# Sparse attention followed by a spectral mix: weight tiles of two modes in one transfer, strided rows of two batches in one transfer, and six modes' real parts in loads of 40 and 24 rows

## The chip, the cores and the metric

The kernel runs on one core of one Trainium2 chip. The metric is device time in microseconds (us) of one execution, as the median of several executions. "Before" is the kernel as it stood, "after" the kernel with the change.

## What is computed

The reference has two parts. Attention over `q`, `k`, `v` of shape 8 x 8 x 576 x 64 (batch, head, position, width): heads 0 to 3 see the last 32 positions (local), heads 4 to 7 see every 32nd position up to their own (strided). The result, as rows of 512, goes through a spectral layer with 64 complex weight matrices of 512 x 512 and a real one, `w_ch`:

```
X = np.fft.rfft(x, axis=1)                       # x: 8 x 576 x 512, out of the attention
Yr = einsum('bmd,mde->bme', Xr, w_r) - einsum('bmd,mde->bme', Xi, w_i)   # 64 modes m
Yi = einsum('bmd,mde->bme', Xr, w_i) + einsum('bmd,mde->bme', Xi, w_r)
y = np.fft.irfft(Y, n=S, axis=1)
u = x + y
return u + np.maximum(u @ w_ch, 0.0)
```

All inputs lie in HBM as 32-bit floats. The two weight arrays alone are 2 x 64 x 512 x 512 x 4 bytes = 134 MB; all that the profile counts as read is 163 MB.

## The kernel before, in words

**Order of the work.** One program runs on TensorE (PE), VectorE (DVE), ScalarE (ACT), GpSimd (POOL) and SyncE (SP). The order of the instructions on each engine is the order in which the Python code emits them; nothing reorders them. The stages are:

1. Strided heads (loop at line 741, 8 batches): transposes, scores, softmax, values, and half of the forward transform (`dft`, line 497). The weight tiles that have room are fetched ahead.
2. Local heads (loop at line 770, 8 batches), with the first pass of the modes between the pieces: `mode(0, m)`, m = 0 to 63, for the upper 256 of the 512 input columns.
3. Second pass of the modes, `mode(1, m)`, m = 0 to 63, for the lower 256 columns. Between the modes stand pieces of other work (`turn`, `premix`, `spec`): about one piece a mode at first, two a mode for the ten modes m = 51 to 60 (`LATE`, line 835). Modes 61 to 63 are emitted at line 948.
4. Last stage (loop at line 956): 36 units of output rows. `v_rows` (line 888) makes a row block on TensorE and ScalarE into a tile `rl`, `u_rows` (line 907) adds in VectorE into a tile `osb`, and SP sends it to HBM.

**A weight tile.** The text below counts tiles from 0 to 127: tile 64 x pass + m. A tile is `[128, 4, 512]` in 16-bit floats. Rows 0 to 63 hold the real part, rows 64 to 127 the imaginary part. Each part is one transfer of 64 rows, 8 KB read and 4 KB written a row (line 190), so a tile takes two transfers, one for `w_r` and one for `w_i`; mode 0 has no imaginary part and takes one. `mode` (line 532) does 16 small matmuls on the tile and then calls `w_fetch()` (line 551), which emits the transfers of the next tile that is not yet fetched.

**Buffers.** The pool `pw` has 11 buffers of one tile each (`NWBUF`, line 27), used in turn. Six further tiles (`GUEST`, line 169) lie in memory that is used for something else later (Y0, X0, YT). In the last stage `rl` and `osb` take turns in the same 11 buffers (lines 895 and 914).

**Queue.** The loads of weights, `q`, `k`, `v` and `w_ch` are all issued by POOL, on one queue, in the order of emission: 315 transfers in all. The program has eight completion semaphores for this queue and uses them in turn, so a transfer isn't issued before the one eight places ahead of it has landed. "Lane" below means one of those eight.

**Strided rows.** `load_str` (line 214) loads 72 rows of 8 KB for each batch and each of `v`, `q`, `k`: 64 rows in one transfer per batch, and the last 8 rows of two batches together in one. That makes 24 transfers of 64 rows and 12 of 8 x 2 rows. They go into a ring of 12 slots, three a batch, so batch b + 4 takes the place of batch b.

Of the kernel before, what the change touches and what calls it, by code (L numbers as in the profile page):

```python
# [10 lines left out]
FP = mybir.dt.float32  # L11
F16 = mybir.dt.float16
# [6 lines left out]
DM = 512  # L19
NM = 64  # L20
# [3 lines left out]
JG = [(0, 6), (6, 11), (11, 16)]  # L24
SCALE = float(1.0 / np.sqrt(D))
NEG = -30000.0
NWBUF = 11


def _host_consts():  # L30
# [49 lines left out]
def kernel(  # L80
# [10 lines left out]
    nc = tc.nc  # L91
# [3 lines left out]
    big = ctx.enter_context(tc.tile_pool(name="big", bufs=1))  # L95
# [5 lines left out]
    def psum_pools(**bufs):  # L101
        pctx.close()
        for n, c in bufs.items():
            pss[n] = pctx.enter_context(
                tc.tile_pool(name="ps_" + n, bufs=c, space=PSUM)
            )

    def psum(kind, half=False):
        if half:
            return pss[kind].tile([128, 1024], F16, tag=kind, name=kind)  # L110
        return pss[kind].tile([128, 512], FP, tag=kind, name=kind)
# [16 lines left out]
    def const_load(eng, *which):  # L128
        for n in which:
            eng.dma_start(cs[n][:, 0 : hosts[names.index(n)].shape[1]], drams[n])  # L130
# [13 lines left out]
    def spectra_tile(n):  # L144
        if n == "X0":
            Xh[0] = big.tile([128, 4, B, 2, NM], F16, tag=n, name=n)
        else:
            YS[n] = big.tile([128, 4, 4, 16, 16], F16, tag=n, name=n)

    xb = [px.tile([128, 11, 256], F16, tag="xb", name="xb") for _ in range(B)]  # L150

    pw = ctx.enter_context(tc.tile_pool(name="pw", bufs=NWBUF))
    actx = ctx.enter_context(ExitStack())
# [3 lines left out]
    ring = pat.tile([128, 12, 2048], F16, name="ring")  # L157
# [8 lines left out]

    GUEST = {3: ("Y0", 0), 4: ("Y0", 1), 5: ("X0", 0), 6: ("X0", 1)}
    GUEST |= {15: ("YT", 0), 16: ("YT", 1)}  # L170
    guests = {}
    w_tiles = []
    w_chs = {}

    def w_fetch(n=1):
        for _ in range(n):
            i = len(w_tiles)
            if i >= 2 * NM:
                return
            half, m = 1 - i // NM, i % NM  # L180
            if i in GUEST:
                n, j = GUEST[i]
                if j == 0:
                    guests[n] = big.tile([128, 2, 4, DM], F16, tag=n, name="wt")
                wt = guests[n][:, j]
            else:
                wt = pw.tile([128, 4, DM], F16, tag="w", name="wt")

            for ri, src in enumerate([moe_w_r, moe_w_i] if m else [moe_w_r]):
                nc.gpsimd.dma_start(  # L190
                    wt[ds(64 * ri, 64)],
                    src[m, ds(256 * half, 256), :].rearrange("(p c) e -> p c e", c=4),
                )
            w_tiles.append(wt)

    def w_ch_fetch():
        w_ch = pw.tile([128, 4, DM], F16, tag="w", name="w_ch")
        nc.gpsimd.dma_start(w_ch, moe_w_ch.rearrange("(c p) e -> p c e", p=128))
        w_chs["n"] = w_ch

# [3 lines left out]
    SRC = {2: v, 0: q, 1: k}  # L204
    SLOT = {2: 0, 0: 1, 1: 2}

    def str_in(b, vi):
        return ring[0:72, 3 * (b % 4) + SLOT[vi], :]
# [2 lines left out]
        t = ring[:, ds(2 * (b % 6), 2), :].rearrange("p n x -> p (n x)")  # L211
        return t[:, ds(1152 * vi, 1152)]

    def load_str(b):
        for vi in (2, 0, 1):
            nc.gpsimd.dma_start(
                str_in(b, vi)[0:64],
                SRC[vi][b, 4:8].rearrange("h (c r) d -> (h c) (r d)", r=32)[0:64],
            )
            if b % 2 == 0:  # L220
                n = 3 * (b % 4) + SLOT[vi]
                nc.gpsimd.dma_start(
                    ring[64:72, n : n + 4 : 3, :],
                    SRC[vi][b : b + 2, 4:8].rearrange(
                        "b h (c r) d -> (h c) b (r d)", r=32
                    )[64:72],
                )

    def load_loc(*bs):
        for b in bs:  # L230
            if b >= B:
                return
            for vi in (2, 0, 1):
                nc.gpsimd.dma_start(
                    loc_in(b, vi),
                    SRC[vi][b, 0:4].rearrange("h (cb i) d -> (h cb) (i d)", i=18),
                )
# [294 lines left out]
    def mode(slot, m):  # L532
        half = 1 - slot
        mi, mg = m % 8, m // 8
        if mi == 0:
            ypt[slot] = psum("y")
        yp = ypt[slot]
        yv = yp.rearrange("p (m e x) -> p m e x", m=8, e=4)
        wt = w_tiles[slot * NM + m]
        pr = ds(0, 128 if m else 64)  # L540
        for e in range(4):
            for c in range(4):
                nc.tensor.matmul(  # L543
                    yv[:, mi, e, :],
                    wt[pr, XC[c], ds(128 * e, 128)],
                    Xh[half][pr, c, :, :, m],
                    start=(c == 0),
                    stop=(c == 3),
                )
        if slot or m not in GUEST:  # L550
            w_fetch()
        ends = {7: 8}
        if slot and mg == 7:
            ends = {5: 6, 7: 2}
        if mi in ends:
            n = ends[mi]
            m0 = mi + 1 - n
            part = (
                slice(None),
                slice(None),  # L560
                mg // 2,
                slice(None),
                ds(8 * (mg % 2) + m0, n),
            )
            src = yp.rearrange("p (m e x) -> p e x m", m=8, e=4)[:, :, :, ds(m0, n)]
            if slot == 0:
                if m == 7:
                    spectra_tile("Y0")
                nc.scalar.activation(out=YS["Y0"][part], in_=src, func=ACTF.Copy)
            else:  # L570
                nc.vector.tensor_tensor(
                    out=YS["YT"][part], in0=src, in1=YS["Y0"][part], op=AluOp.add
                )
# [117 lines left out]


    psum_pools(tp=3, sc=3, av=2)
    load_str(0)
    const_load(nc.scalar, "cI", "cM6", "cM5", "cFs")
    load_str(1)
    const_load(nc.sync, "cMl", "cFl", "cA")
    load_str(2)
    w_fetch(2)

    def str_front(b):
        return [
            lambda: str_v(b, 0), lambda: str_v(b, 1),
            lambda: str_v(b, 2), lambda: str_q(b, 0),
            lambda: str_back(b, 0),
            lambda: str_back(b, 1), lambda: str_q(b, 1),
            lambda: str_k(b, 0),
            lambda: str_k(b, 1), lambda: str_k(b, 2),
        ]

    def loc_front(b):
        if b >= B:
            return [lambda: None] * 8
        return [
            lambda: loc_turn(b, 0, 0), lambda: loc_turn(b, 0, 1),
            lambda: loc_turn(b, 1, 0), lambda: loc_turn(b, 1, 1),
            lambda: loc_turn(b, 2, 0), lambda: loc_turn(b, 2, 1),
            lambda: loc_back(b, 0), lambda: loc_back(b, 1),
        ]
# [19 lines left out]
                )  # L739
    SPLIT = [0, 2, 4, 5, 7, 8, 10]  # L740
    for b in range(B):
        if b < 5:
            load_str(b + 3)
        load_loc(*[(), (), (), (), (0,), (1, 2), (3,), (4, 5)][b])
        w_fetch([3, 3, 2, 2, 2, 1, 1, 1][b])
        front = str_front(b + 1) if b + 1 < B else loc_front(0)
        for t in range(6):
            str_scores(b, t)
            if b > 0:
                if t < 2:  # L750
                    str_values(b - 1, 4 + t)
                elif t == 2:
                    dft(b - 1, 1)
            if t >= 2:
                str_values(b, t - 2)
            for w in front[SPLIT[t] : SPLIT[t + 1]]:
                w()
        if b == 1:
            nc.vector.memset(PL[:, 0:PS0], 0.0)
# [10 lines left out]
    for b in range(B):  # L770
# [12 lines left out]
        n = 0  # L783
        nm = NMODES[b]
        for mi in range(nm):
# [3 lines left out]
            n = upto  # L789
# [5 lines left out]
    ptr = ctx.enter_context(tc.tile_pool(name="ptr", bufs=1))  # L795
# [37 lines left out]
    n = 0  # L833
# [3 lines left out]
    for m in range(NM - 3):  # L837
# [7 lines left out]
        n = upto  # L845
# [11 lines left out]
    held, vps, ups, rls, osbs = {}, {}, {}, {}, {}  # L857
# [5 lines left out]
    def pool_adds(b, t):  # L863
        if (b, t) in ((0, 1), (B - 1, 3)):
            return False
        return t in (1, 3, 4) or (b, t) in ((2, 2), (4, 2))
# [21 lines left out]
    def v_rows(i):  # L888
        b, t = units[i]
        if i not in vps:  # L890
            v_early(i)
        vp = vps.pop(i)
        rows_of(b, t, vp, zzs, False)
        if t % 2 == 0:
            rls[b, t] = rls[b, t + 1] = pw.tile([128, 2, DM], FP, tag="w", name="rl")
        rl = rls[b, t][:, t % 2, :]
        nc.scalar.activation(out=rl, in_=vp, func=ACTF.Relu)  # L897
        if pool_adds(b, t):
            nc.gpsimd.tensor_tensor(out=rl, in0=rl, in1=x_rows(b, t), op=AluOp.add)  # L899
# [48 lines left out]
    for m in range(NM - 3, NM):  # L948
        mode(1, m)
# [6 lines left out]
    for i in range(len(units)):  # L956
        v_rows(i)
        b, t = units[i]
# [42 lines left out]
```

The softmax here doesn't subtract the row's maximum and nothing guards it: scores larger than these inputs give would overflow.

## Time and profile before

| what | value |
|---|---|
| median of 10 runs | 437.89 us (437.27 to 439.97) |
| the profiled execution | 437.64 us, of which the span of instructions 435.9 us |
| PE busy | 337.8 us, 78% of the span |
| DVE, ACT, POOL busy | 216.1, 188.2, 186.6 us |
| POOL's queue | 26800 packets, 81.29 MB written, 94.8% of 16 DMA engines' span |
| HBM read, written | 163.22 MB, 9.44 MB |

The span is what the profile shows of one execution; the 1.7 us around it are start and end. "Busy" for a DMA queue is the time that packets took, summed over 16 DMA engines. A packet is one contiguous piece: here mostly a row of 8 KB read as 32-bit floats and written as 4 KB of 16-bit floats. A line such as `POOL wt L190 <- DMA wt<-in_moe_w_i_dram: 57.7, 104, 1.8` reads: before instructions of line 190 that write the tile `wt`, POOL sat idle for 57.7 us in all, in 104 places, at most 1.8 us, and a DMA that brings `w_i` ended the wait.

### The profile page before, as it was taken

Reading aid. Unit: us, or ns where it says so; the run is one execution under the profiler, and the core shown is the slowest. Engines: PE = TensorE matmul, PEld = TensorE weight load, DVE = VectorE, ACT = ScalarE, POOL = GpSimd, SP = SyncE. Lnnn points to the kernel's source line nnn. Section 1 sums busy time; section 2 is a strip of 40 time slices with the busy share of each in tenths; the row PEclk is TensorE's granted clock in tenths of the full one; section 3 lists DMA queues with packets and bytes.
Section 4 is the critical chain, followed back from the end, with each engine's and each line's share of the span. In section 5 each row is a group of like instructions: output and inputs, shape, how many; then the busy total and the mean of one; then the engine's idle time right before and its main releaser. Section 6 shows DMA issues by size and latency. Waiting matters only on the chain.

```text
span 435.9 us, 12328 instructions
## 1 busy us (share of the span) xinstructions
PE 337.8 (78%) x5289; PEld 243.3 (56%) x5289; DVE 216.1 (50%) x466; ACT 188.2 (43%) x353; POOL 186.6 (43%) x339
## 2 busy tenths in 40 slices
PE   1988778679897779889755567768585859988994
PEld 1866667558776567677644345445444545554441
DVE  2786887935335243353411034354244442764895
ACT  1585777744554345444431202133122312443882
POOL 6545454333444343444343444344344344420883
PEclk9996999979868766685885558698778687999999
DMA  9999999999999999999999999999999999991687
GB/s 172 204 212 211 212 211 211 211 210 211 212 211 214 211 209 212 212 212 212 212 209 213 211 212 212 212 211 211 201 211 211 212 212 212 211 211 37 265 322 281
DMA packets 31094, 92.20 MB, mean 212 GB/s; under 512 B 6144, under 2 KB 7168, under 8 KB 31040
## 3 DMA queue, kind: packets, MB, share of 16 engines
q0 software_dynamic: 26800, 81.29, 94.8%
q1 hardware_dynamic: 3440, 9.46, 5.8%
q10 hardware_dynamic: 800, 0.67, 0.6%
q8 instruction: 42, 0.69, 0.6%
q14 instruction: 12, 0.10, 0.1%
HBM read 163.22 MB, written 9.44 MB: 396 GB/s over the span
## 4 chain that ended last, share of the span: by engine, by line
DMA 59%; PE 22%; DVE 9%; issue 4%; ACT 2%; POOL 1%; DVEq 0%; POOLq 0%
DMA wt<-in_moe_w_i_dram 51%; DMA wt<-in_moe_w_r_dram 5%; PE y L543 3%; PE sc L641 2%; DVE kz L288 2%; PE u L684 2%; PE v L684 2%; PE v L886 2%; DVE xb L246 2%; DMA ring<-in_k_dram 2%; DMA ring<-in_q_dram 2%; PE sc L510 2%; ACT X L256 1%; PE tp L391 1%; DVE rec L245 1%
## 5 line engine op out<-in xcount | busy, mean ns | idle before, releaser
L543 PE MATMUL y<-X,wt 128*128 128x16 f16 (+1 forms) x2048 | 83.0, 192 | 59.1 <-DMA wt<-in_moe_w_i_dram 56.6
L190 POOL DMA_DIRECT2D wt<-in_moe_w_r_dram x128 | 65.8, 514 | 120.0 <-DMA wt<-in_moe_w_r_dram 30.3
L543 PEld LDWEIGHTS <-wt 128*128 128x128 f16 (+1 forms) x2048 | 72.5, 103 | 72.9 <-issue 54.7
L190 POOL DMA_DIRECT2D wt<-in_moe_w_i_dram x126 | 64.7, 513 | 67.8 <-DMA wt<-in_moe_w_i_dram 49.6
L650 ACT ACTIVATE v<-sc 128x512 f16<-128x512 f32 x32 | 19.0, 597 | 85.9 <-PE sc L641 85.9
L641 PE MATMUL sc<-w_cp,xT 128*128 128x512 f16 (+1 forms) x160 | 51.5, 452 | 0.5 <-DVE xT L613 0.4
L467 ACT ACTIVATE PL<-sc 128x480 f16<-128x480 f32 (+1 forms) x48 | 27.6, 579 | 46.9 <-PE sc L453 46.5
L651 DVE COPY xo<-tp 128x512 f16<-128x512 f16 x32 | 22.1, 692 | 40.1 <-PE tp L649 40.1
L246 DVE TENSOR_TENSOR xb<-av,rec 90x256 f16<-90x256 f32 (+2 forms) x80 | 36.0, 450 | 2.7
L245 DVE RECIPROCAL rec<-av 90x4 f32<-90x4 f32 (+2 forms) x80 | 14.7, 184 | 40.5 <-PE av L482 28.1
L398 DVE COPY qT<-tp 128x576 f16<-128x576 f16 x16 | 12.0, 758 | 41.4 <-PE tp L391 38.5
L256 ACT ACTIVATE v<-tp 128x640 f16<-128x640 f16 (+1 forms) x24 | 19.4, 808 | 20.9 <-PE tp L425 17.2
L391 PE MATMUL tp<-cI_s,ring 64*64 64x64 f16 x864 | 26.2, 211 | 1.7 <-DVE kz L398 0.9
L356 ACT ACTIVATE PL<-sc 90x360 f16<-90x360 f32 (+1 forms) x48 | 22.9, 490 | 10.4 <-PE sc L349 9.8
L899 POOL TENSOR_TENSOR rl<-rl,xo 128x512 f32<-128x512 f32 x16 | 18.3, 1156 | 18.2 <-ACT rl L897 17.9
L916 DVE TENSOR_TENSOR osb<-u,rl 128x512 f32<-128x512 f32 x36 | 23.6, 689 | 2.6 <-PE u L684 1.3
L391 PEld LDWEIGHTS <-ring 64*64 64x64 f16 x864 | 20.8, 123 | 6.5 <-issue 3.8
L437 PE MATMUL sc<-cMl_s,cI_s 128*128 128x480 f16 (+1 forms) x48 | 22.4, 467 | 1.6 <-ACT X L256 1.6
L453 PE MATMUL sc<-qT,kz 128*128 128x160 f16 (+1 forms) x160 | 22.6, 267 | 0.9 <-issue 0.9
L281 PE MATMUL tp<-cI_s,ring 72*128 72x72 f16 x256 | 15.1, 207 | 10.4 <-DMA ring<-in_v_dram 7.7
L641 PEld LDWEIGHTS <-xT 128*128 128x128 f16 (+1 forms) x160 | 14.8, 110 | 14.9 <-issue 7.2
L453 PEld LDWEIGHTS <-kz 128*128 128x128 f16 x160 | 16.2, 116 | 11.1 <-issue 8.3
(98 smaller groups left out, 650.7 us busy)
## 6 DMA issues: line engine op xcount, KB each, us to landing
wt<-in_moe_w_r_dram POOLq DMA_DIRECT2D x128, 256.0 KB, 9.4
wt<-in_moe_w_i_dram POOLq DMA_DIRECT2D x126, 256.0 KB, 9.6
out_dram<-osb SPq DMA_DIRECT2D x14, 512.0 KB, 2.7
ring<-in_v_dram POOLq DMA_DIRECT2D x8, 288.0 KB, 10.2
ring<-in_q_dram POOLq DMA_DIRECT2D x8, 288.0 KB, 10.5
ring<-in_k_dram POOLq DMA_DIRECT2D x8, 288.0 KB, 10.6
ring<-in_v_dram POOLq DMA_DIRECT2D x8, 256.0 KB, 8.4
ring<-in_q_dram POOLq DMA_DIRECT2D x8, 256.0 KB, 8.5
```

The source lines that it names most:

```text
L190: nc.gpsimd.dma_start(wt[ds(64 * ri, 64)], src[m, ds(256 * half, 256), :].rearrange("(p c) e -> p c e", c=4),)
L246: nc.vector.tensor_tensor(out=dst, in0=val.rearrange("p h (q c) -> p h c q", c=4), in1=rec[0:n, 0:pieces] .to_broadcast((n, pieces, 64)) . ...
L256: nc.scalar.activation(out=out, in_=in_, func=ACTF.Copy)
L356: nc.scalar.activation(out=PS[0:n, ds(POFF[t], 4 * n)], in_=scp[0:n, 0 : 4 * n], func=ACTF.Exp, scale=SCALE,)
L391: nc.tensor.transpose(tp[ds(64 * hp, 64), ds(64 * i, 64)], qn[ds(64 * hp, 64), ds(64 * (9 * g + i), 64)], idn[ds(64 * hp, 64), ds(64 * hp, ...
L437: nc.tensor.matmul(scp[:, 0 : n * times].rearrange("p (h x) -> p h x", h=times), idn, mask_rows("cMl", n, times), start=True, stop=False,)
L453: nc.tensor.matmul(scp[:, ds(col, n)], kzs[par][:, hp, ds(s0, 128)], qTs[par][:, ds(s0, n)], start=False, stop=(i == len(todo) - 1),)
L467: nc.scalar.activation(out=dst, in_=src, func=ACTF.Exp, scale=SCALE)
L543: nc.tensor.matmul(yv[:, mi, e, :], wt[pr, XC[c], ds(128 * e, 128)], Xh[half][pr, c, :, :, m], start=(c == 0), stop=(c == 3),)
L641: nc.tensor.matmul(vp[pr, :], xT[:, ch, cols], w_chs["cp"][:, ch, :], start=(ch == 0), stop=(ch == 3),)
L651: nc.vector.tensor_copy(out=xo[pr].rearrange("p (h q c) -> p h q c", h=2, c=4), in_=tp[pr, 0:512].rearrange("p (h c q) -> p h q c", h=2, c=4),
L916: nc.vector.tensor_tensor(out=osb[:, t % 2, :], in0=up, in1=rls[b, t][:, t % 2, :], op=AluOp.add)
```

## The change

Four edits, all in the loads and the buffers:

- **Pairs of modes.** `w_fetch` brings two modes at a time. A tile is `[128, 2, 4, 512]`; the two modes' real parts are one transfer of 64 x 2 rows, the imaginary parts another. Exceptions: mode 0 still has no imaginary part; the last two pairs (tiles 124 to 127) come in single transfers, in the order real, real, imaginary, imaginary. `NWBUF` is 5 (pairs), three pairs are guests (tiles 2-3, 4-5, 14-15), and `mode` calls `w_fetch` after odd modes only.
- **Short loads.** In the pairs that begin with tiles 28, 62 and 96 (`CUT`), the real parts come in four transfers: 40 rows and 24 rows for each of the two modes.
- **Strided rows.** From batch 2 on, the 64 rows of two batches are one transfer (batches 2-3, 4-5, 6-7); the loads of batches 4 to 7 are emitted in loop passes 1 and 3 in place of 1 to 4.
- **Room.** `w_ch` has a buffer of its own. `rl` takes turns in two buffers named `rl` and in the two of `xT`; `osb` has the five buffers of `pw`.

Of POOL's 315 transfers 193 are left: weights 254 to 141, strided rows 36 to 27; the 24 local loads and `w_ch` stay. The instructions of TensorE stay in the same order.

```
-NWBUF = 11
+NWBUF = 5
...
-    GUEST = {3: ("Y0", 0), 4: ("Y0", 1), 5: ("X0", 0), 6: ("X0", 1)}
-    GUEST |= {15: ("YT", 0), 16: ("YT", 1)}
+    GUEST = {1: "Y0", 2: "X0", 7: "YT"}
+    CUT = (28, 62, 96)
...
-            if i in GUEST:
-                n, j = GUEST[i]
-                if j == 0:
-                    guests[n] = big.tile([128, 2, 4, DM], F16, tag=n, name="wt")
-                wt = guests[n][:, j]
+            if i // 2 in GUEST:
+                wt = big.tile([128, 2, 4, DM], F16, tag=GUEST[i // 2], name="wt")
             else:
-                wt = pw.tile([128, 4, DM], F16, tag="w", name="wt")
-
-            for ri, src in enumerate([moe_w_r, moe_w_i] if m else [moe_w_r]):
-                nc.gpsimd.dma_start(
-                    wt[ds(64 * ri, 64)],
-                    src[m, ds(256 * half, 256), :].rearrange("(p c) e -> p c e", c=4),
-                )
-            w_tiles.append(wt)
+                wt = pw.tile([128, 2, 4, DM], F16, tag="w", name="wt")
+            for ri, src in enumerate((moe_w_r, moe_w_i)):
+                dst = wt[ds(64 * ri, 64)]
+                rows = src[m : m + 2, ds(256 * half, 256), :].rearrange(
+                    "m (p c) e -> p m (c e)", c=4
+                )
+                dst = dst.rearrange("p m c e -> p m (c e)")
+                ones = range(2)
+                if ri and not m:
+                    ones = [1]
+                elif i < 2 * NM - 4 and (ri or i not in CUT):
+                    nc.gpsimd.dma_start(dst, rows)
+                    continue
+                for j in ones:
+                    cuts = (0, 40, 64) if i in CUT and not ri else (0, 64)
+                    for a, z in zip(cuts, cuts[1:]):
+                        nc.gpsimd.dma_start(dst[a:z, j], rows[a:z, j])
+            w_tiles.extend((wt[:, 0], wt[:, 1]))
...
-    def load_str(b):
+    def load_str(b, nb):
         for vi in (2, 0, 1):
-            nc.gpsimd.dma_start(
-                str_in(b, vi)[0:64],
-                SRC[vi][b, 4:8].rearrange("h (c r) d -> (h c) (r d)", r=32)[0:64],
-            )
+            n = 3 * (b % 4) + SLOT[vi]
+            two = ring[:, n : n + 4 : 3, :]
+            src = SRC[vi][b - b % 2 : b - b % 2 + 2, 4:8].rearrange(
+                "b h (c r) d -> (h c) b (r d)", r=32
+            )
+            if nb == 2:
+                nc.gpsimd.dma_start(two[0:64], src[0:64])
+            else:
+                nc.gpsimd.dma_start(ring[0:64, n, :], src[0:64, b % 2])
             if b % 2 == 0:
...
+                nc.gpsimd.dma_start(two[64:72], src[64:72])
...
-        if slot or m not in GUEST:
+        if m % 2 and (slot or m // 2 not in GUEST):
             w_fetch()
...
-        if b < 5:
-            load_str(b + 3)
+        if b in (1, 3):
+            load_str(b + 3, 2)
...
-        w_fetch([3, 3, 2, 2, 2, 1, 1, 1][b])
+        w_fetch([2, 1, 1, 1, 1, 1, 0, 0][b])
...
-            rls[b, t] = rls[b, t + 1] = pw.tile([128, 2, DM], FP, tag="w", name="rl")
+            n = len(rls) // 2 % 2
+            rl = ptr.tile([128, 2, 576], FP, tag="xT" if n else "rl", bufs=2, name="rl")
+            rls[b, t] = rls[b, t + 1] = rl[:, :, 0:DM]
```

More of the change, by code (lines that the diff above doesn't have):

```diff
@@ L165 @@
     v16 = [pat.tile([128, 12, 132], F16, name=f"v16_{i}") for i in range(2)]
-    GUEST = {3: ("Y0", 0), 4: ("Y0", 1), 5: ("X0", 0), 6: ("X0", 1)}
-    GUEST |= {15: ("YT", 0), 16: ("YT", 1)}
-    guests = {}
+    GUEST = {1: "Y0", 2: "X0", 7: "YT"}
+    CUT = (28, 62, 96)
     w_tiles = []
     w_chs = {}
+    w_ch = big.tile([128, 4, DM], F16, name="w_ch")
     def w_fetch(n=1):
@@ L180, in w_fetch @@
             half, m = 1 - i // NM, i % NM
-            if i in GUEST:
-                n, j = GUEST[i]
-                if j == 0:
-                    guests[n] = big.tile([128, 2, 4, DM], F16, tag=n, name="wt")
-                wt = guests[n][:, j]
-            else:
-                wt = pw.tile([128, 4, DM], F16, tag="w", name="wt")
-            for ri, src in enumerate([moe_w_r, moe_w_i] if m else [moe_w_r]):
-                nc.gpsimd.dma_start(
-                    wt[ds(64 * ri, 64)],
-                    src[m, ds(256 * half, 256), :].rearrange("(p c) e -> p c e", c=4),
-                )
-            w_tiles.append(wt)
+            if i // 2 in GUEST:
+                wt = big.tile([128, 2, 4, DM], F16, tag=GUEST[i // 2], name="wt")
+            else:
+                wt = pw.tile([128, 2, 4, DM], F16, tag="w", name="wt")
[3 more added lines that the diff above has]
+                    "m (p c) e -> p m (c e)", c=4
+                )
+                dst = dst.rearrange("p m c e -> p m (c e)")
[10 more added lines that the diff above has]
+            w_tiles.extend((wt[:, 0], wt[:, 1]))
     def w_ch_fetch():
-        w_ch = pw.tile([128, 4, DM], F16, tag="w", name="w_ch")
         nc.gpsimd.dma_start(w_ch, moe_w_ch.rearrange("(c p) e -> p c e", p=128))
@@ L212, in loc_in @@
         return t[:, ds(1152 * vi, 1152)]
-    def load_str(b):
+    def load_str(b, nb):
         for vi in (2, 0, 1):
-            nc.gpsimd.dma_start(
-                str_in(b, vi)[0:64],
-                SRC[vi][b, 4:8].rearrange("h (c r) d -> (h c) (r d)", r=32)[0:64],
-            )
+            n = 3 * (b % 4) + SLOT[vi]
+            two = ring[:, n : n + 4 : 3, :]
+            src = SRC[vi][b - b % 2 : b - b % 2 + 2, 4:8].rearrange(
+                "b h (c r) d -> (h c) b (r d)", r=32
+            )
+            if nb == 2:
+                nc.gpsimd.dma_start(two[0:64], src[0:64])
+            else:
+                nc.gpsimd.dma_start(ring[0:64, n, :], src[0:64, b % 2])
             if b % 2 == 0:
[L221 to L226, printed above, removed]
-                )
+                nc.gpsimd.dma_start(two[64:72], src[64:72])
     def load_loc(*bs):
@@ L693 @@
     psum_pools(tp=3, sc=3, av=2)
-    load_str(0)
+    load_str(0, 1)
     const_load(nc.scalar, "cI", "cM6", "cM5", "cFs")
-    load_str(1)
+    load_str(1, 1)
     const_load(nc.sync, "cMl", "cFl", "cA")
-    load_str(2)
-    w_fetch(2)
+    load_str(2, 2)
+    w_fetch()
     def str_front(b):
```

## The prediction

> **What bounds the kernel now.** I read the page's slices first. The DMA row and the rate below it:
>
> ```profile
> DMA  9999999999999999999999999999999999991687
> GB/s 172 204 212 211 212 211 211 211 210 211 212 211 214 211 209 212 212 212 212 212 209 213 211 212 212 212 211 211 201 211 211 212 212 212 211 211 37 265 322 281
> q0 software_dynamic: 26800, 81.29, 94.8%
> q8 instruction: 42, 0.69, 0.6%
> ```
>
> For 36 of 40 slices (392 of 436 us) the DMA engines are full at an even rate. Only then comes the last stage, about 40 us of output. So the end is set by when the stream of loads ends, and by what TensorE still has to do then. Next, the chain of waits between 340 and 400 us (start, length, what):
>
> ```profile
> 347.38 9.63 DMA wt<-in_moe_w_i_dram
> 357.29 9.63 DMA wt<-in_moe_w_i_dram
> 367.05 0.65 PE y L543 x16
> 367.70 0.86 PE sc L641 x4
> 368.79 0.98 PE sc L641 x4
> 370.88 0.69 DVE xT L593
> ```
>
> Two things are to be seen. A link of the DMA chain is 357.29 - 347.38 = 9.91 us. It spans eight transfers, one turn of the eight lanes, so a transfer of 64 rows costs 9.91 / 8 = 1.239 us. And the chain leaves the DMA at 367 us: from tile 115 (second pass, mode 51) on, TensorE and VectorE are the bound, with two pieces of other work a mode. The waits of the window 366 to 398 us say the same, three columns being total, times, longest:
>
> ```profile
> POOL wt L190 <- DMA wt<-in_moe_w_i_dram: 4.2, 9, 0.5
> PE y L543 <- DMA wt<-in_moe_w_i_dram: 0.3, 1, 0.3
> ```
>
> Last, the DMA view of 380 to 398 us, in slices of 0.45 us:
>
> ```profile
> GB/s 228 200 209 200 228 173 264 164 246 191 237 182 228 209 191 246 173 255 173 237 200 219 200 218 228 218 218 100 118 91 118 91 127 82 91 36 0 0 0 0
> ```
>
> From slice 28 (392.2 us) to 396.3 us the rate is half. Eight of the 16 engines are done 4 us before the other eight, and a tile has landed only when all 16 are done. The completion times of single transfers, which the trace holds too (16 a transfer), show how this grows: first to last engine 1.7 us at 50 us, 2.9 us at 125 us, 4.4 us at 240 us, 4.2 us at 389 us, where the late ones are eight engines, 2.2 to 4.0 us behind the others. The 42 instruction fetches of queue 8 explain it: 16 KB each, at 8 KB in 0.304 us (below) 0.6 us each, 42 x 0.6 = 25 us, or 3.2 us on each of eight engines.
>
> **What the skill says.** The Trainium skill's "DMA: Bandwidth & Descriptors", section "Why a DMA increments its semaphore by 16 and not by 1", says that on this queue all 16 engines post a completion for every transfer, whatever its shape. The trace agrees: 315 transfers and 5232 packets of 4 bytes, which is 315 x 16 and 192 more, 16 for each of the twelve 8-row loads. Its section "Anatomy of one DMA" calls that bubble tiny, about one cycle. The trace disagrees: on one engine rows start 0.3045 us apart, and 0.0215 us lie between a completion packet and the next row (4 x 0.3042 + 0.0215 = 1.238, the price above). The trace decides. The first section also gives the placement: a transfer runs on the largest number of engines up to 16 that divides the row count, from a cursor that moves on. The 8-row loads agree: after three of them, at 40 us, eight engines are 0.6 us (2 rows) behind where they stood, and after the next three, at 62 us, that is level again. By this rule 40 rows go to ten engines and 24 to twelve; no run here shows such a load.
>
> **The change part by part.**
>
> *Fewer transfers.* 315 - 193 = 122 completions fewer on each engine: 122 x 0.0215 = 2.62 us. The twelve short loads probably bring one more packet each, like the 8-row loads: 12 x 0.0215 = 0.26 back. Net -2.36 us on the stream, about 93% of it (2.2) before tile 115. The bytes don't change. That the engines, not a shared path, set the pace is seen at 393 to 395 us, where eight engines run alone and rows still take 0.324 us, as before; so a saved packet is saved time. Bounds: 0 (if the saved slot goes to waiting) to -2.6.
>
> *40 and 24 rows.* Both are multiples of 8: 40 = 8 x 5, 24 = 8 x 3. If such a load goes to eight engines, as the 8-row loads do, one half gets 5 rows a mode and the other 3 in place of 4 and 4. Which half is which: at 40 us the eight engines that took the first and third 8-row load of a set of three stand together 0.6 to 1.1 us behind the first, five stand within 0.5, and three, which fetches have delayed, at 1.4 to 1.7; so the late three belong to the other half, with the five. Twelve 8-row loads bring the cursor back, so 40 goes to the early half, 24 to the late one. Six modes x 1 row x 0.304 = 1.83 us less on the late half, 1.83 more on the early one; its lead of 2.2 to 4 us covers that. By the page's rule (10 and 12 engines, cursor 6 on after each mode) no engine gains or loses over 2 rows net and the late half still has unrelieved engines: 0. If instead rows are dealt from the first engine on, 3 and 2 an engine, 12 engines get 5 rows a mode, late ones among them: +1.83. I take -1.83, since a split at 8 x 5 and 8 x 3 fits the one placement that the trace shows for a short load; ends -1.83 and +1.83.
>
> *Waiting for the partner.* An even mode's tile now lands with the odd one's, 2 x 1.239 = 2.48 us later. Up to tile 113 TensorE has idle time for it (it waited 56.6 us for `w_i` in all), and queued behind the waiting matmul is only work that the odd mode's wait held up before. From 114 on there is none. The trace has landed / first matmul: tile 114 364.45 / 364.81, tile 116 369.41 / 369.92, tile 118 374.37 / 374.71. Tile 114 starts 2.48 + 0.14 - 0.36 = 2.26 us later against the stream (0.14 from landing to first matmul, as on all waiting tiles), and 116 and 118 then find their tiles there (118: 374.37 + 2.48 + 0.14 = 376.99, 2.28 late). All that follows shifts by about 2.25. The last four tiles come singly and had 1.05 to 4.2 us of slack; they don't bind. Cost +2.25 us; bounds +1.5 (ScalarE and VectorE catch up during the wait) to +2.5.
>
> *Buffers.* Five pairs in place of 11 tiles: when a pair is freed, four pairs (8 transfers, 8 x 2.46 = 19.7 us of stream) are queued; issue and freeing take about 4 us of it. In the first pass the next fetches wait for modes 1, 7, 9, 11 in place of 0, 1, 2, 7: mode 7 ends at 106.1 us, and the stream has earlier transfers until 112. No gap, 0 us; without that cover each us of delay is one us of stream.
>
> *Strided pairs.* Batch 4 to 7 rows land later: v of batch 4 at 36.9 + 3.7 = 40.6 us, used at 43.8; k at 46.5, used at 50; k of batch 6 at 64.5, used about 67.7. Cover about 3 us; 0 us. Even 3 us lost there would vanish: TensorE is bound by itself until tile 23 and waits for loads from 136 us on. POOL's issues (0.51 us a row load, 0.78 for 512 rows) get fewer.
>
> *`rl`, `osb`.* A `rl` buffer is taken again after four tiles, 7 to 8 units, and freed 4 units earlier at least; `osb` after five tiles, 9 units of about 1 us, with 2.7 us from issue to landing. 0 us; up to +1 if VectorE lags.
>
> **Sum.** Stream at tile 115: -2.2 - 1.83 = -4.0. Partner wait +2.25. Net -1.8 us. The profiled execution took 437.64 (span 435.9 and 1.7 around it), so 435.8; it lies 0.25 below the median of the runs, so 436.1 against the median. I predict 436.0.
>
> **The rivals.**
>
> A, the sum above: 436.0, own range 434.3 to 437.2. Chance 0.56.
>
> B, the 40 and 24 rows don't balance (ten and twelve engines): stream -2.2, wait +2.25, so nothing: 437.8. For it: the page's rule; against it: nothing in the trace. Chance 0.22. It is also the case that the short loads don't do what they say.
>
> C, slower: the short loads fall on late engines. Stream -2.2 + 1.83 = -0.4, and the partner wait then decides: +2.25 - 0.4 = +1.8, 439.6. The place is tiles 114 to 118; it decides as soon as the stream gains less than 2.25 us. Against it: the early half took the first 8-row load. Chance 0.11.
>
> D, the partner wait doesn't bind, since the bound stretch from 367 us absorbs it (VectorE works off its copies during the wait; TensorE waits for VectorE there in six groups, 3.8 us in all): nearly all of -4.0 stays: 433.9. Against it: TensorE is busy 27.8 of 32 us from 366 to 398. Chance 0.11.
>
> **How the numbers follow.** A measurement of this kernel tells about 0.3% (1.3 us) from no change: faster is below 436.6, slower above 439.2. Faster: D whole and four fifths of A, 0.57. Same: the rest of A and B, 0.32. Slower: C, 0.11. The range 433.8 to 438.6 takes in A, B and D and leaves C out. A's own range stands above.
>
> **What would show it.** Right: queue 0 has 26800 - 122 x 16 + 12 x 16 = 25040 packets; the chain's DMA links, eight transfers, are 2 x 9.91 - 8 x 0.0215 = 19.65 us long; the half rate at the stream's end shrinks from 4 us to below 1; the last weight lands near 392 instead of 396.6; an even mode waits before tiles 114 to 118. Wrong: half rate of 4 us or more (B, C); no wait at 114 to 118 (D); links of 19.8 us, which would void the saved packets; gaps in the DMA row before 390 us, which would void the buffers' cover; or the time from the last mode to the end, 37.6 us before, changed by over 1 us.

## The result, and the profile after

After takes 441.87 us (median of 9 runs, 440.3 to 443.09), before 438.06 (31 runs): ratio 1.0082, 95% interval 1.0066 to 1.0099. It is slower by 0.8%; the forecast was 436.0 and faster. The profiled execution of after took 441.27 us, its span 439.5, against 437.64 and 435.9.

The page's DMA rows of after, as shown for before in the prediction:

```profile
DMA  9999999999999999999999999999999999970687
GB/s 169 204 209 213 212 212 212 211 210 212 214 212 213 212 214 214 213 213 214 215 207 210 214 213 213 214 214 213 198 214 213 213 213 215 211 149 4 265 318 279
q0 software_dynamic: 24944, 81.28, 93.9%
q8 instruction: 41, 0.67, 0.6%
```

The packets went down by 1856, and most slices are a little faster than before (213 to 214 in place of 211 to 212): that is the saved completions. But slices 20 and 28 (counted from 0; 220 and 308 us) show 207 and 198; before had 209 and 201 there, and after without its short loads (e1 below) has 212 and 214:

```profile
GB/s 171 208 211 212 212 214 213 211 210 213 214 211 214 214 214 214 214 213 213 213 212 213 213 214 213 214 214 212 214 214 213 214 213 215 212 172 13 267 315 287
```

Next, the chain of waits from 340 us on (start, length, what):

```profile
332.91 19.38 DMA wt<-in_moe_w_i_dram
352.57 19.38 DMA wt<-in_moe_w_i_dram
372.08 0.65 PE y L552 x16
...
378.87 0.86 PE sc L650 x4
...
389.77 1.40 PE sc L650 x3
```

A link of eight transfers is 352.57 - 332.91 = 19.66 us, as forecast (19.65). The chain leaves the DMA at 372.08, at mode 116, where before it left at 367.05, at mode 115. Mode 116 started at 369.92 before: 2.16 later. Up to mode 122 the shift stays (387.97 for 385.82). Then a group of four `sc` matmuls that took 0.86 us at 378.87 takes 1.40 at 389.77, with only three of its records: the granted clock from 390 to 400 us is 0.84, where before had 1.00. The view by stretches shows it (stretch, length, then busy time of PE, PEld, DVE, ACT and POOL with the number of instructions, granted clock, DMA share, GB/s), first before, then after:

```profile
390.00:400.00 10.00, 8.49 (x108) 5.17 (x105) 3.62 (x6) 2.58 (x5) 0.00 (x0) 1.00 0.43 86
390.00:400.00 10.00, 9.21 (x92) 5.32 (x91) 3.46 (x5) 2.98 (x5) 0.00 (x0) 0.84 0.30 60
```

The last mode ends at 401.95, before 398.33, which is 2.16 + about 1.4 for the clock; from there to the end it is 37.55 us (before 37.6). The waits of 366 to 398 us (total, times, longest):

```profile
POOL wt L199 <- DMA wt<-in_moe_w_i_dram: 0.9, 1, 0.9
...
PE y L552 <- DMA wt<-in_moe_w_i_dram: 0.7, 2, 0.5
```

TensorE waits for `w_i` twice here, 0.17 us at mode 114 (its tile landed at 367.01) and 0.50 at mode 116 (371.95); mode 118 starts 0.13 us after its tile landed. These are the forecast places. Last, the DMA view of after from 380 to 398 us, to be compared with that of before in the prediction:

```profile
GB/s 200 237 191 219 218 191 237 218 228 173 237 200 219 200 209 209 182 218 191 219 137 155 173 200 173 91 109 73 82 64 73 64 64 100 36 36 9 18 0 0
```

From slice 25 (391.3 us) on, half of the rate or less, and a tail below a third: some engines end 6 us behind others. The prediction wanted this to shrink below 1 us.

So, the clock apart, what follows tile 115 went as forecast, and the stream didn't: tile 115 landed at 367.01 us (before 366.91), where the sum had it 4.0 us earlier. The question is what ate 4 us of stream.

### The profile page after: what moved, and what is told of

It is laid out like the page before. It is cut to its first block, busy times and chain, and to the rows that moved or that the text cites. A ratio compares the mean times of both kernels' runs of the same rounds, so it can differ in the third digit from the quotient of the medians.

```text
span 439.5 us, 12075 instructions
## 1 busy us (share of the span) xinstructions
PE 337.8 (77%) x5289; PEld 241.6 (55%) x5289; DVE 215.2 (49%) x466; ACT 188.0 (43%) x353; POOL 133.5 (30%) x217
## 3 DMA queue, kind: packets, MB, share of 16 engines
q0 software_dynamic: 24944, 81.28, 93.9%
## 4 chain that ended last, share of the span: by engine, by line
DMA 77%; PE 15%; issue 3%; DVE 2%; ACT 1%; DVEq 0%; POOL 0%; POOLq 0%; ACTq 0%
DMA wt<-in_moe_w_i_dram 43%; DMA wt<-in_moe_w_r_dram 16%; DMA ring<-in_k_dram 11%; DMA ring<-in_q_dram 7%; PE sc L650 3%; PE y L552 2%; PE u L693 2%; PE v L693 2%; PE v L895 2%; DMA ring<-in_v_dram 1%; DVE yy L683 1%; DVE xT L602 1%; PE u L916 1%; PE tp L658 1%; PE tp L400 1%
## 5 line engine op out<-in xcount | busy, mean ns | idle before, releaser
L199 POOL DMA_DIRECT2D wt<-in_moe_w_r_dram x59 | 34.7, 587 | 117.3 <-PE y L552 36.5
L199 POOL DMA_DIRECT2D wt<-in_moe_w_i_dram x60 | 35.3, 589 | 71.7 <-DMA wt<-in_moe_w_i_dram 51.2
L650 PE MATMUL sc<-w_cp,xT 128*128 128x512 f16 (+1 forms) x160 | 52.6, 458 | 0.4 <-DVE xT L622 0.4
L254 DVE RECIPROCAL rec<-av 90x4 f32<-90x4 f32 (+2 forms) x80 | 14.7, 184 | 43.2 <-PE av L491 31.9
L519 PEld LDWEIGHTS <-xb 108*128 108x128 f16 (+2 forms) x176 | 16.9, 114 | 10.9 <-issue 5.2
## 6 DMA issues: line engine op xcount, KB each, us to landing
ring<-in_q_dram POOLq DMA_DIRECT2D x3, 512.0 KB, 14.7
```

The lines of the kernel that those rows point to most:

```text
L199: nc.gpsimd.dma_start(dst, rows)
L650: nc.tensor.matmul(vp[pr, :], xT[:, ch, cols], w_chs["cp"][:, ch, :], start=(ch == 0), stop=(ch == 3),)
```

## The experiments

Each kernel was timed beside the kernel before, whose median was 438.2 us (e1 to e4), 437.97 (e5 to e8) and 438.66 (e9 and e10), so ratios compare best. In the table, the completion times of tile 115's last transfer (16, one from each engine) are told by their mean and their last; the last decides when the tile can be used. The mean is late when engines stand idle, last minus mean is large when their loads are uneven. The trace doesn't name the engines; "the first engine" below is the earliest of the 16 times. The mean also holds the start of each execution: at tile 27, ahead of every short load, after and e10 are already 0.55 and 0.51 us behind e1, e9 is level with it, and e7 is 0.42 ahead, with the same transfers up to there. So differences of half a microsecond in this table mean little.

| kernel | median us | ratio to before, 95% | tile 115: mean | last | last - mean |
|---|---|---|---|---|---|
| before | 438.06 | 1 | 364.54 | 366.91 | 2.37 |
| after | 441.87 | 1.0082 (1.0066 to 1.0099) | 363.13 | 367.01 | 3.88 |
| e1_no_cut | 437.33 | 0.9985 (0.9972 to 0.9999) | 361.32 | 364.75 | 3.43 |
| e2_cut48 | 440.56 | 1.0062 (1.0041 to 1.0084) | 363.56 | 366.33 | 2.77 |
| e3_single | 437.36 | 0.9976 (0.9965 to 0.9988) | 362.20 | 365.40 | 3.20 |
| e4_single_cut48 | 441.83 | 1.0072 (1.0052 to 1.0092) | 364.23 | 366.88 | 2.65 |
| e5_before_cut40 | 440.40 | 1.0051 (1.0032 to 1.0070) | 366.32 | 368.31 | 1.99 |
| e6_before_cut48 | 441.94 | 1.0098 (1.0071 to 1.0126) | 368.92 | 370.00 | 1.08 |
| e7_even_cut32 | 437.93 | 1.0001 (0.9987 to 1.0014) | 361.14 | 364.61 | 3.47 |
| e8_cut40_pairs | 438.58 | 1.0012 (0.9999 to 1.0025) | 361.37 | 364.61 | 3.24 |
| e9_spread_cut40 | 441.29 | 1.0059 (1.0041 to 1.0076) | 362.40 | 367.87 | 5.47 |
| e10_even_cut16 | 447.46 | 1.0191 (1.0167 to 1.0216) | 371.60 | 373.61 | 2.01 |

**e1: after without the short loads.**

```
-    CUT = (28, 62, 96)
+    CUT = ()
```

> The changed kernel without the short loads: real parts of tiles 28-29, 62-63 and 96-97 in one transfer a pair again. Theory 1 (short loads are dealt from the first engine on, three rows an engine for 40, two for 24, so 12 or 13 engines, the late ones among them, get 5 rows a mode in place of 4): the stream at tile 115 lands 1.8 + 0.3 = 2.1 us earlier, 367.0 to about 364.9, and the kernel takes about 439.8 us. Theory 2 (the placement is harmless, the time goes into the wait of the even modes and the buffers): no change, about 441.9. In both, the gap from first to last engine grows by less than 0.5 us at tiles 28, 62 and 96 here.

437.33 us, 4.5 us below after and below both numbers. Against before, tile 115 lands 2.16 us earlier and the last weight 2.29 earlier (394.35 for 396.64): the saved completions. (The forecast of 2.2 and 2.36 was for after; e1 has 131 transfers fewer, which at 0.0215 us would make 2.8 at the end.) Mode 116 nevertheless starts at 369.80, before 369.92: the wait for the partner takes all of it, as forecast. So the other parts of the change come to nearly nothing, and the short loads are the loss.

The mean moved more than the last engine, by 3.22 us, and most of the difference is a loss that the kernel before had and the prediction overlooked: its stream wasn't even. POOL came to this issue late (the bracket: idle before it, and what ended that):

```profile
308.58 0.52 POOL L190 DMA_DIRECT2D wt<-in_moe_w_r_dram  x1 [3.88 <-PE y L543]
```

When the issue ended, the first engine had 0.25 us of work left; eight engines completed this transfer 0.8 to 1.4 us late, 0.6 us in the mean of 16. That is the 201 of slice 28. A smaller case near 157 us cost 0.2 us. In e1 POOL stood for 3.3 us with its lane free near 235 us, and the first engine still had 6.46 us queued: pairs of modes hold twice the work in eight lanes. The late engines, which decide when a tile can be used, lost nothing by it in either kernel.

**e2: 48, 8 and 8 rows in place of 40 and 24.**

```
-                    cuts = (0, 40, 64) if i in CUT and not ri else (0, 64)
+                    cuts = (0, 48, 56, 64) if i in CUT and not ri else (0, 64)
```

> The changed kernel with the six real parts in loads of 48, 8 and 8 rows in place of 40 and 24. Theory 1: 48 rows are 3 on each of 16 engines, 8 rows are 1 on each of the first eight, so the first eight engines get 5 rows and the others 3. The instruction fetches are on the other eight, so the late half gains 6 x 0.304 = 1.8 us against the kernel without short loads, less about 0.4 for 12 to 24 more completions: about 438.2 us, and the half rate at the stream's end shrinks to under 2 us. Theory 2 (placement harmless): 441.9. If the late engines are the first eight, 441.5 or more.

440.56, between the two. The engines do end closer together, yet the stream is late: its mean is 2.24 us behind e1's. Something other than uneven rows delays it; slice 21 of its page (230 us) has 190 GB/s, e1's 213.

**e3 and e4: single transfers from tile 104 on, so that no mode waits for a partner; e3 without short loads, e4 with 48, 8 and 8 rows.**

```
+            if i >= SINGLE:
+                for j in range(2):
+                    for ri in range(2):
+                        dst, rows = part(ri)
+                        nc.gpsimd.dma_start(dst[:, j], rows[:, j])
```

> The changed kernel without short loads, and with tiles 104 to 127 in single transfers in the order real, imaginary of one mode, then of the next. Theory 1 (partner wait): tiles 114, 116, 118, 120, 122 land with no partner, the 2.2 us of waits before them go, 24 - 4 = 20 more completions cost 20 x 0.0215 = 0.4 us: against the kernel without short loads 1.8 us less, about 438.0. Rival (the partner wait is absorbed, the loss is in the buffers of rl and osb or in a lower clock of TensorE): as the kernel without short loads, about 439.8 or 441.9.

> Both remedies: single transfers from tile 104 on and the six real parts in loads of 48, 8 and 8 rows. Theory 1: 438.0 - 1.8 + 0.4 = 436.6 us, under the kernel before (438.0). Rival (effects don't add, since the clock or the last stage sets the end): 438 or more.

e3: 437.36, the lowest ratio of all kernels here. Mode 116 starts at 369.01, 0.8 us before e1's, not 2.2: the stream carries more transfers again (tile 115 at 365.40), and TensorE is now bound from mode 113 on. e4: 441.83, far off the first number; the short loads cost 4.5 us here too, so it isn't the wait for the partner that makes them dear.

**e5 and e6: the kernel before with short loads alone.** Two theories are set against each other from here on: P, that the uneven rows delay the late engines, and Q, that short loads fill the eight lanes with little work, so that queues run dry.

```
-                nc.gpsimd.dma_start(
-                    wt[ds(64 * ri, 64)],
...
+                cuts = (0, 40, 64) if i in (28, 29, 62, 63, 96, 97) and not ri else (0, 64)
+                for a, z in zip(cuts, cuts[1:]):
+                    nc.gpsimd.dma_start(dst[a:z], rows[a:z])
```

(e6 has 0, 48, 56, 64.)

> The kernel before with one thing added: the real parts of tiles 28, 29, 62, 63, 96, 97 in loads of 40 and 24 rows, nothing else of the change. Theory P (the engines that carry the short loads are to blame: 40 rows lie on 13 engines by 3 and 24 rows on 12 by 2, the same engines each time): the late engines get up to 6 rows, 1.8 us, more, so 438.1 + 1.8 = 440, with a spread at the last tiles of about 6 us in place of 4.2. Theory Q (the eight lanes are to blame: short loads leave fewer rows queued on each engine): the lanes of this kernel hold only 8 x 1.24 us, so the queues run dry more than in the kernel after: 441.5 or more, with dips of the rate in the slices of 120, 220 and 320 us. The prediction's own step (balance) would give 436.3.

> The same with 48, 8 and 8 rows, which balanced the engines in the kernel after (spread 2.5 to 3.5 us at the end). P: the late engines gain, so 437 to 438.1, no slower than before. Q: six or twelve short transfers in a row hold the eight lanes with little work, and the queues run dry: 440 or more, with dips of the rate where the short loads lie.

Both slower, 440.4 and 441.94. The size of e5 fits P, its trace doesn't: the spread got smaller than before (last - mean 1.99 for 2.37), and the mean is 1.78 us late. e6 refutes P as the whole cause: its engines end closer together than those of before, and 4.38 us of mean are lost. The rates of e5's page dip at 230 us (slice 21), to 176; the 200 of slice 29 may be in part the late issue that before has there too:

```profile
GB/s 175 210 213 211 212 210 212 210 210 212 213 211 211 207 212 212 212 212 213 212 207 176 211 213 212 212 213 212 207 200 211 212 213 211 212 213 42 260 331 270
```

**e7: cuts of 32 and 32 rows; e8: 40 and 24 rows, both modes in one transfer.**

```
-                    cuts = (0, 40, 64) if i in CUT and not ri else (0, 64)
+                    cuts = (0, 32, 64) if i in CUT and not ri else (0, 64)
```

```
+                if i in CUT and not ri:
+                    for a, z in ((0, 40), (40, 64)):
+                        nc.gpsimd.dma_start(dst[a:z], rows[a:z])
+                    continue
```

> The kernel after with cuts of 32 and 32 rows in place of 40 and 24: as many transfers in the same places, each by 2 rows on all 16 engines. P: no engine gets more than another, so this is the kernel without short loads and 12 packets on each engine, 437.3 + 0.3 = 437.6. Q: as many lanes hold half loads as in the kernel after, so nearly its time, 441 to 442.

> The kernel after with the 40 rows of both modes in one transfer (40 x 2 rows) and the 24 rows of both in another: two transfers where the kernel after has four, the same rows on the same engines if the placement goes by the first dimension (6 rows on 13 engines, 4 on 12). P: the kernel after again, 441.5 to 442. Q: half as many lanes are held by short loads, so a half or less of the 4.5 us: 438 to 439.5.

e7 has as many short loads as after in the same places, and is level with before: 437.93; P's number, not Q's. Against e1 it is 0.16% (0.7 us) slower by ratio, with intervals that overlap. In its trace the engines move on by about 0.63 us with each load, as 2 rows and a completion should. e8 is at 438.58, Q's number; but its rows don't lie as after's do (at its third place the latest engine gets none of the 40 rows: its completions are at 316.64 and 316.82 us), so e8 doesn't tell P from Q. With e5 and e6 for Q and e7 for P, neither was enough alone. How they can meet is seen on POOL. Its timeline in after, at the second place (start, length, what, and in brackets the wait before it and what ended it):

```profile
215.34 0.53 POOL L204 DMA_DIRECT2D wt<-in_moe_w_r_dram  x1 [2.13 <-DMA wt<-in_moe_w_i_dram]
217.56 0.52 POOL L204 DMA_DIRECT2D wt<-in_moe_w_r_dram  x1 [1.69 <-DMA wt<-in_moe_w_r_dram]
220.00 0.51 POOL L204 DMA_DIRECT2D wt<-in_moe_w_r_dram  x1 [1.92 <-DMA wt<-in_moe_w_i_dram]
222.44 0.50 POOL L204 DMA_DIRECT2D wt<-in_moe_w_r_dram  x1 [1.93 <-DMA wt<-in_moe_w_r_dram]
225.24 0.61 POOL L199 DMA_DIRECT2D wt<-in_moe_w_i_dram  x1 [2.29 <-DMA wt<-in_moe_w_i_dram]
```

Each issue waits about 2 us for a lane, which a full pair's transfer frees every 2.46 us. Each short load fills that lane with far less work. The engine that is ahead gets no rows at all from these four loads (four completions 0.16 to 0.17 us apart), so it loses 2.0 to 2.7 us of queue each time: at the end of these five issues it has 9.60, 7.55, 5.30, 3.04 and 0.30 us left. The last of them ends at 225.85 and completes on the first engine at 230.65, 4.80 us later, of which eight rows are 2.46; with 0.30 us queued, this engine loses 2 us (its next completion comes 4.50 us after the last, not 2.46). In e7 the same five numbers are 10.49, 8.77, 6.99, 5.04 and 2.44: the rows that every engine gets keep it fed. From tile 27 to 115, after's mean falls behind e1's by 0.1 us at the first place, 0.4 at the second and 0.8 at the third. This draining is theory D of the last two experiments.

**e9: short loads in six pairs in place of three, one mode each; e10: four loads of 16 rows, one row on each engine.**

```
-    CUT = (28, 62, 96)
+    CUT = (28, 44, 62, 78, 96, 108)
...
-                    cuts = (0, 40, 64) if i in CUT and not ri else (0, 64)
+                    cuts = (0, 40, 64) if i in CUT and not ri and not j else (0, 64)
```

```
-                    cuts = (0, 40, 64) if i in CUT and not ri else (0, 64)
+                    cuts = (0, 16, 32, 48, 64) if i in CUT and not ri else (0, 64)
```

> The kernel after with the six short-load pairs spread out: in six pairs (tiles 28, 44, 62, 78, 96, 108) only the first mode's real part comes as 40 and 24 rows, the second's as 64. The rows that fall on each engine are those of the kernel after in all, but each place has two short loads in place of four. Theory D (a lane that is freed by a transfer of 2.46 us and filled with a short one drains the queue of the engine that gets no rows by 2.46 - 0.17 = 2.3 us; four in a row drain 9.2 of the 9.6 us that are queued): here 2 x 2.3 + 1.2 = 5.8 us are drained, so no engine runs dry and no slice dips at the places; only the uneven rows are left. With the rows as in the kernel after that is up to +1.8 on the late engines: 437.4 to 439.2, spread at the end 6.7 to 8.5 us. Theory P (only the uneven rows cost, nothing runs dry): the kernel after again, 441.5.

> The kernel after with four cuts of 16 rows (one row on each of the 16 engines) in place of 40 and 24: eight short loads in a row in each of three places, no engine gets more rows than another. Theory D: eight times 2.46 - 0.33 = 2.1 us are drained, 17 us, more than the 10.4 that the first engine has queued and about what the last has (10.4 + 5.5); so the first engines run dry for some 6 us, the last ones for 1 to 2 us, in each place: dips in slices 13, 21 and 29, a spread that shrinks to below 4 us, and 1 to 1.5 us a place at the stream's end: 440.5 to 442. Theory P: no uneven rows, so 437.4 + 0.5 for 24 more transfers = 437.9, no dips, spread 6.5 us.

e10 shows the draining by itself: no uneven rows, and 447.46 us. Its first engine's queue goes 12.3, 11.2, 9.1, 7.0, 4.8, 2.8, 0.6, -0.8 us over the eight short loads of the first place, about 2.1 us each after the first, as D has it (below zero it is already idle); then the engines stop, and only then come close together. The DMA view of e10 from 142 to 154 us (slices of 0.3 us) shows the hole:

```profile
GB/s 205 219 150 137 178 164 123 96 96 109 82 55 219 68 178 55 123 150 218 218 191 205 218 150 219 205 205 218 205 218 205 205 219 191 218 218 218 218 218 218
```

D's direction held, its size was too small: 10.3 us of mean lost to e1, not 3 to 4.5. Part of that is a stop of POOL at the second place: the lane was free at 233.59 and the issue came at 236.80, with no wait named.

e9 was to show the uneven rows by themselves, and does so only in part. At its first place no queue falls below 6.4 us and the rate holds, yet at tile 115 the last engine is 5.47 us behind the mean, e1's 3.43: 2.04 more, where D had +1.8. The result, 441.29, is P's number, above D's range. By ratio it is 0.23% (1.0 us) below after, though the intervals overlap. And near 233 us, behind its third place, the first engine is down to 0.59 us and then loses 1.8 us, where D had no engine run dry. From tile 27 to 115 the mean falls 1.08 us behind e1's, in after 1.27. So spreading the loads out removed little of the lost mean and let the lag grow by 1.6 us over after's. In after both are at work, and its lag is only 0.45 above e1's. That they feed on each other (an engine that runs dry stops gaining its lead; and the larger the lead, the less that engine has queued when the last one frees a lane) fits the queues above, but no run shows it, and how much of after's loss each would cost alone stays open.

## Why the prediction was wrong

**40 and 24 rows: this step failed.** It said: "I take -1.83, since a split at 8 x 5 and 8 x 3 fits the one placement that the trace shows for a short load". Measured from e1 to after at tile 115: +2.26 us, of which 0.49 stood already at tile 27, ahead of the first short load. So the short loads cost about +1.8 us in place of -1.83: 1.27 in the mean of the engines, 0.5 in the lag of the last one behind it. (At the last weight it is +3.39, 397.74 for 394.35; the 1.1 more came after tile 119, where there are no short loads.) The placement was wrong: in e9's first place a load of 40 rows gives three rows to thirteen engines (0.87 to 0.99 us, but 0.68 and 1.35 on two), one row (0.37) to one and none (0.17, 0.18) to two; a load of 24 rows gives two rows to twelve (0.52 to 0.90) and none to four (0.16, 0.17). That is neither eight engines nor ten. The Trainium skill's "DMA: Bandwidth & Descriptors", section "Why a DMA increments its semaphore by 16 and not by 1", gives it as an exception for this kind of queue: some direct copies put the row count over 16, rounded up, on each engine. The prediction used the section's rule and its own analogy with the 8-row loads; a placement like the exception's it had only as the end +1.83, which is rival C. (Each engine's step is the best match of two sorted lists of completions, so these counts are a fit, not a reading.)

And a right placement wouldn't have been enough: rows moved from one engine to another leave the mean where it was, and the mean lost 1.27 us, of which nine more transfers explain 0.2. The sum counted what a short load does to the rows of an engine, and nothing for the lane that it holds. Eight lanes hold 8 x 2.46 = 19.7 us of work in after, of which the first engine has 9.6 us left at the first short load of the second place (10.5 in e7). Rival C priced the placement, and no case priced the lane; that C's +1.83 is near the measured size is in part luck.

**Fewer transfers: right.** e7, with after's own 193 transfers and even rows, lands tile 115 2.30 us and the last weight 2.45 us earlier than before, give or take the half microsecond by which starts differ; forecast -2.2 and -2.36. The skill's same page, section "Rules for kernel authors", advises joining small transfers into large ones; these runs agree, with 2.45 / 122 = 0.020 us an engine for each transfer saved, transfers of 256 KB being joined. It isn't 25040 packets but 24944: only six of the twelve short loads bring 16 more.

**Waiting for the partner: right.** +2.16 us at mode 116 for +2.25, of which 0.10 is tile 115's own delay. With the stream's gain gone it is all that is left ahead of the slow clock, so the place where after loses is that of rival C.

**Buffers, strided pairs, `rl` and `osb`: right, 0.** e1 holds them all, and saved completions and partner wait explain it to 0.3 us of span (435.5 for 435.9). POOL now waits longer for TensorE to free a buffer (36.5 us for 14.7 in the whole run), but the engines have their 10 us queued behind that.

**The sum.** Before 437.64, partner +2.16, stream +0.1 rather than -4.0 (the next tiles show it in the 2.16), clock about +1.4: 441.2; measured 441.27. Between e1 and after, mode 116 is 2.28 us later and the clock again about 1.4: 3.7 of the 4.0 us between their spans (435.5 and 439.5). The clock wasn't in the sum. Whether the short loads have part in it is open: the profiled runs of e3 (387 us) and e8 (397 us) show such a slow stretch too, those of before, e1, e7 and e9 don't have it between 367 us and their last mode. That it lifts the medians of after and e2 above what their streams say is a guess.

## What to carry to other kernels

Splitting a transfer to shift rows between DMA engines pays for a completion lane with less work than it held; what an engine has queued when the lane comes free, less the 2 us or so that a new transfer takes to take effect, is what may be drained before it idles. Look at the rows per engine in the completion times of one such load before building on a balance; 32 and 32, the same rows for every engine, cost nothing clear of the noise; 40 and 24 cost 1% of the kernel; and four times 16, the same rows again but in more and shorter loads, cost 2%. Joining transfers was worth its price, but look at who waits for the joined half: here it gave back all of the gain, and single transfers for the last 24 tiles (e3, ratio 0.9976) have the lowest ratio of the study, though e1's interval overlaps theirs.

## What the runs showed of the hardware

- An engine that a transfer gives no row still posts its completion, 0.16 to 0.18 us after the one before (after, e9); with rows the completion adds 0.0215 us (before).
- In e10, with all engines idle, the first row starts 0.70 us after the end of POOL's issue (237.99 for 237.29), and the first rows of the next transfer take up to 1.07 us where a row takes 0.324 in a full stream of before.
- POOL stood still for 3.1 to 3.3 us from about 234 us on with its lane free, in after, e1, e7, e8, e9 and e10; the profile names no cause.
- A late issue empties queues by what they hold: a stop of 3.9 us before an issue left the first engine 0.25 us with eight single transfers outstanding (before), one of 3.3 us left it 6.46 with eight pairs (e1).
